# A kernel ordered by a planner: one place per batch for every stage, batches 0 to 2 in two groups, six result places, five for bt

## The chip, the cores and the metric

The kernel runs on one core of one Trainium2 chip. The metric is its device time in microseconds (us), the median of several runs. The core's engines have queues of their own and meet through semaphores: PE (TensorE) multiplies matrices, ACT (ScalarE), DVE (VectorE) and POOL (GpSimd) work on elements, SP (SyncE) issues all transfers between memory (HBM) and the core's buffers. Every queue is worked off in its order: an instruction that waits holds all that stand behind it on the same engine.

## The reference

Two attention steps with 32 inducing points, and a feed-forward stage whose nonlinearity is `h - tanh(h)`:

```python
def mab(q, kv):
    s = scale * (q @ kv.transpose(0, 2, 1))
    s = s - s.max(-1, keepdims=True)
    a = np.exp(s)
    a /= a.sum(-1, keepdims=True) + 1e-09
    return a @ kv
h = mab(I, x)                       # I: 32 x 128, for each of B = 4 batches; x: 4 x 12480 x 128
attn = mab(x, h)                    # 4 x 12480 x 128
...
h = x @ w_in                        # x: attn as 49920 x 128; w_in: 128 x 2048
g = h - np.tanh(h)
return (g @ w_out).astype(np.float32)   # w_out: 2048 x 128
```

Inputs and output are float32, but for `w_in` and `w_out`, which are 64-bit floats.

## The kernel before, in words

**Tiling.** A batch's 12480 rows are cut into seven tiles, s = 0 to 6: six of 1920 rows (four segments of 480, one for each quarter of the 128 partitions) and a last one of 960. `x` is in memory twice, transposed (`xT`, a load of 128 x 1920) and as rows (`xn`, a load of 128 x 1920; the last half tile comes from `xl` with 64 partitions). An input tile is 960 KB, half a result tile 480 KB.

**First stage of a batch** (`first`, `attend`). For each tile: load `xT`; scores against the inducing points on PE (L322, `ps_m<-xT,indT_sb`); on DVE a copy into `s1` with the row's maximum (L348). When all tiles of a group are done, the maximum is turned and spread (L355 to L367, the last writes `nb`). Then for each tile: exponential on ACT (L398), 32 x 32 transposes on DVE (L402, `et`), and 15 small matmuls that accumulate `h` in the PSUM tile `bank` (L409, `bank<-xn,et`). The rows `xn` of a tile are loaded (L391), or, for the tiles in `TURNED`, made on PE from `xT` (L381) and copied by ACT (L387): no transfer, but the same buffer. A batch that `SPLIT` names is worked in two groups of tiles, each with its own maximum, which are put together at the end with a few more small steps (`hA`, `f`); otherwise all seven tiles are one group, and no exponential starts before the last tile's maximum. At the end the sums are taken (L449), `h` is normed and folded (L465 or L461, L468) and copied to `hT` (L470).

**The map of a batch** (`linear`). The feed-forward stage is brought down to one 32 x 128 map for each batch, kept four times in `P4`: `hT` times `w_in` (L491), a copy to `M4` (L494), turned and centred (L503), a series and squares, `W` times `w_out` (L545), fold (L549), copy to `P4` (L551). Bounds are kept beside, and `bound` (the guard) decides at the end by them whether this was exact enough (`limit`); if not, a general path would run, which it doesn't here.

**Second stage** (`second`, `b_chain`). For each tile: scores against `hT` on PE (L322, `ps_m<-xT,hT`), transposes on DVE into `be` (L594), maximum (L596), difference on POOL (L601), exponential on ACT (L603), on POOL the two halves' sum into `bs` (L608), on DVE the sum (L611) and its reciprocal (L614), product on POOL (L615), transposes into `bt` (L618), on PE the matmuls with `P4` (L643, `o<-bt,P`), two copies out of PSUM (L649, into `ot` on ACT; for the last batch into an `xT` place, on ACT or DVE), and two stores (L653).

**The weights.** `w_in` and `w_out` come as four pieces each into `xn` places (L277) and are made float32 there by steps on DVE (L281 to L298), ACT (L284, L295) and POOL (L302).

**The order.** Nothing is scheduled at run time. `Plan.add` records each step with an engine, a cost, the buffers that it reads and writes, and a priority `pri`; `Plan.order` plays the program through with these costs: an engine that is free takes the ready step of the lowest priority whose buffers have a free place (`PLACES` says how many each kind has). The result is written out as the fixed order of each engine. So the numbers in `ORD`, `PLACES`, `SPLIT`, `TURNED`, the lags and the costs set where every instruction stands. `FILL` says how much of PE's idle time in the plan is filled with matmuls of no use (L734, `bank<-ident`).

In `ORD`, `first` and `second` are the starting priorities of each batch's two stages, `fs` and `ss` the step from tile to tile, `lx` and `ln` how far the loads of `xT` and `xn` go ahead, `lns` their step, `turn` and `keep` the place of the turned tiles, `base`, `q`, `half` and `late` that of the maximum, the exponentials, the end of the first stage and the bounds, `store` that of the result stores.

## Time and profile before

| what | us |
|---|---|
| median of 3 runs (220.1 to 221.13) | 220.41 |
| the profiled execution's own time | 221.32 |
| its span, first to last instruction | 219.6 |
| PE busy, with weight loads apart | 178.1 (81%) |
| DVE busy | 155.3 (71%) |
| ACT busy | 116.8 (53%) |
| POOL busy | 97.8 (45%) |

HBM reads are 47.46 MB and writes 25.56 MB, 333 GB/s over the span. The granted TensorE clock is 0.911 of full speed on average.

In what follows, PEclk is the share of full TensorE clock that was granted, in tenths for each of 40 slices of the span; the DMA line is the busy share of the 16 DMA engines in the same slices. A timeline row has its start in us, its length in us, engine, line, operation, what it writes and reads, the count, and in brackets the engine's idle time before it with what ended that. PEld is PE's weight loads, which run beside the matmuls. "SPq" is the issue of a transfer on SP, not the transfer.

### The profile page before, as it was taken

The page shows a single profiled execution, that of the slowest core. Times are in us where ns is not written, and L with a number is a line of the kernel's source. Part 1 is how long each engine was busy: PE and PEld are TensorE (multiplying, and loading weights), DVE is VectorE, ACT ScalarE, POOL GpSimd, SP SyncE. Part 2 cuts the span into 40 slices and gives each one's busy share as a digit, 9 for nine tenths or more (in the row PEclk, how much of TensorE's full clock was granted, in tenths as well). Part 3 has the DMA queues.
Part 4 walks back from the last instruction along what each step waited for, and adds up shares of the span by engine and source line. Part 5 has one row for each costly group of instructions (what it writes and reads, how often), then busy time and mean ns, then how long its engine had stood idle before and what let it go on. Part 6 is the DMA issues. An engine that isn't in the chain of part 4 may idle for free.

```text
span 219.6 us, 5239 instructions
## 1 busy us (share of the span) xinstructions
PE 178.1 (81%) x2015; PEld 92.7 (42%) x2015; DVE 155.3 (71%) x402; ACT 116.8 (53%) x229; POOL 97.8 (45%) x138
## 2 busy tenths in 40 slices
PE   7565589848968999995799985998997999799740
PEld 7542244744432467332226651334454434346310
DVE  5799986543697995667388953496979048888960
ACT  2426356930324999385178961367943836648310
POOL 1135414000299643339454641189334245989600
PEclk9979679999999999999699995799999559889995
DMA  5999998799999899999999999599999924609793
GB/s 170 414 417 357 322 405 323 268 292 344 417 421 417 262 416 363 423 405 427 416 411 323 336 419 420 192 358 421 361 381 353 378 113 179 237 36 372 286 400 125
DMA packets 15472, 73.44 MB, mean 334 GB/s; under 512 B 1872, under 2 KB 1872, under 8 KB 15440
## 3 DMA queue, kind: packets, MB, share of 16 engines
q1 hardware_dynamic: 15440, 73.03, 87.3%
q8 instruction: 18, 0.29, 0.5%
q14 instruction: 14, 0.11, 0.2%
HBM read 47.46 MB, written 25.56 MB: 333 GB/s over the span
## 4 chain that ended last, share of the span: by engine, by line
PE 46%; DMA 25%; DVE 12%; ACT 6%; POOL 4%; issue 2%; SPq 1%; ACTq 0%; POOLq 0%; DVEq 0%
PE ps_m L322 17%; DMA xT<-in_xT 14%; PE o L643 10%; PE bank L409 6%; PE ps_m L381 5%; DMA outT<-ot 4%; DMA xn<-in_xl 4%; DMA xn<-in_w_out 3%; PE ps_m L491 2%; ACT xn L387 2%; DVE xT L649 2%; ACT s L398 2%; DVE xn L292 1%; DVE xn L298 1%; PE ps_m L549 1%
## 5 line engine op out<-in xcount | busy, mean ns | idle before, releaser
L601 POOL TENSOR_TENSOR be<-be,bmx 128x480 f32<-128x480 f32 (+1 forms) x25 | 25.2, 1013 | 49.3 <-DVE bmx L596 42.6
L322 PE MATMUL ps_m<-xT,indT_sb 128*32 128x480 f32 x208 | 32.6, 667 | 17.8 <-DMA xT<-in_xT 11.5
L649 ACT COPY ot<-o 128x960 f32<-128x960 f32 x39 | 36.4, 959 | 14.7 <-DMA outT<-ot 7.9
L643 PE MATMUL o<-bt,P 32*128 32x480 f32 x184 | 31.9, 654 | 3.6 <-ACT ot L649 2.9
L615 POOL TENSOR_TENSOR be<-be,brs 128x480 f32<-128x480 f32 (+1 forms) x25 | 24.8, 995 | 21.6 <-DVE brs L614 15.3
L409 PE MATMUL bank<-xn,et 128*32 128x128 f32 (+1 forms) x840 | 30.9, 280 | 4.3 <-DMA xn<-in_xn 2.9
L348 DVE TENSOR_SCALAR_CACHE_REDUCE s<-ps_m 128x480 f32<-128x480 f32 (+1 forms) x28 | 18.2, 650 | 20.4 <-PE ps_m L322 20.4
L409 PEld LDWEIGHTS bank<-xn,et 128*32 128x32 f32 (+1 forms) x840 | 23.8, 111 | 14.5 <-issue 5.9
L322 PE MATMUL ps_m<-xT,hT 128*32 128x480 f32 x208 | 28.0, 604 | 0.2 <-ACT D L507 0.2
L387 ACT COPY xn<-ps_m 128x512 f32<-128x512 f32 (+1 forms) x32 | 17.3, 556 | 11.6 <-PE ps_m L381 11.5
L608 POOL TENSOR_TENSOR bs<-be 128x240 f32<-128x240 f32 (+1 forms) x25 | 17.9, 718 | 10.5 <-ACT be L603 10.4
L734 PE MATMUL bank<-ident 128*128 128x128 f32 x110 | 20.2, 328 | 1.9 <-POOL ident masks.py:199 1.4
L402 DVE STREAM_TRANSPOSE et<-s 128x480 f32<-128x480 f32 (+1 forms) x28 | 18.4, 659 | 3.8 <-ACT s L398 3.8
L594 DVE STREAM_TRANSPOSE be<-ps_m 128x480 f32<-128x480 f32 (+1 forms) x25 | 16.5, 661 | 5.7 <-PE ps_m L322 5.7
L734 PEld LDWEIGHTS bank<-ident 128*128 128x128 f32 x110 | 17.6, 236 | 6.8 <-issue 4.5
L381 PE MATMUL ps_m<-ident,xT 128*128 128x128 f32 x120 | 19.5, 300 | 0.7 <-ACT xn L387 0.5
L398 ACT ACTIVATE s<-s,nb 128x480 f32<-128x480 f32 (+1 forms) x28 | 19.4, 696 | 0.7 <-DVE nb L367 0.5
L381 PEld LDWEIGHTS ps_m<-ident,xT 128*128 128x128 f32 x120 | 14.2, 152 | 10.5 <-issue 3.0
L618 DVE STREAM_TRANSPOSE bt<-be 128x480 f32<-128x480 f32 (+1 forms) x25 | 16.6, 664 | 2.3 <-POOL be L615 2.1
L603 ACT ACTIVATE be<-be 128x480 f32<-128x480 f32 (+1 forms) x25 | 14.9, 604 | 3.9 <-POOL be L601 3.9
L322 PEld LDWEIGHTS ps_m<-xT,indT_sb 128*32 128x32 f32 x208 | 5.8, 117 | 26.0 <-issue 10.9
L596 DVE TENSOR_REDUCE bmx<-be 128x15 f32<-128x480 f32 (+1 forms) x25 | 15.7, 633 | 0.1
(126 smaller groups left out, 226.8 us busy)
## 6 DMA issues: line engine op xcount, KB each, us to landing
xT<-in_xT SPq DMA_DIRECT2D x24, 960.0 KB, 9.3
outT<-ot SPq DMA_DIRECT2D x39, 480.0 KB, 8.6
xn<-in_xn SPq DMA_DIRECT2D x16, 960.0 KB, 10.2
outT<-xT SPq DMA_DIRECT2D x13, 480.0 KB, 3.1
xn<-in_w_in SPq DMA_DIRECT2D x4, 512.0 KB, 5.4
xn<-in_w_out SPq DMA_DIRECT2D x4, 512.0 KB, 6.0
xT<-in_xT SPq DMA_DIRECT2D x4, 480.0 KB, 10.4
xn<-in_xl SPq DMA_DIRECT2D x4, 480.0 KB, 8.1
```

The source lines that it names most:

```text
L322: nc.tensor.matmul(ps[q * m:(q + 1) * m, :SEG], lhsT=w, rhs=row, start=True, stop=True)
L348: nc.vector.tensor_scalar(out=s1.get()[:P, s, :], in0=ps.get()[:P, :SEG], scalar1=1.0, scalar2=None, op0=ALU.mult, op1=ALU.max, accum_out= ...
L381: nc.tensor.transpose(out=pt.get()[:, i * 128:(i + 1) * 128], in_=xT_b[b, s].get()[:, (k + i) * 128:(k + i + 1) * 128], identity=ident)
L387: nc.scalar.copy(out=x.get()[:, k:k + n, :].rearrange("p k c -> p (k c)"), in_=pt.get()[:, :n * 128])
L398: nc.scalar.activation(out=sl, in_=sl, func=AF.Exp, scale=SC, bias=nb.get()[:P], accum_out=sums.get()[:P, s:s + 1])
L402: add("DVE", 0.66, lambda et=et, s=s, P=P: nc.vector.transpose(out=et.get()[:P].rearrange("p k i -> p (k i)"), in_=s1.get()[:P, s, :]), re ...
L409: nc.tensor.matmul(hacc.get()[q * m:(q + 1) * m, :], lhsT=et.get()[:P, k, :], rhs=x.get()[:P, k, :], start=(s == group[0] and k < NQ), sto ...
L601: add("POOL", 1.02, lambda: nc.gpsimd.tensor_tensor(out=be.get()[:P], in0=be.get()[:P], in1=wide(bmx.get()[:P]), op=ALU.subtract), reads=[ ...
L615: add("POOL", 1.02, lambda: nc.gpsimd.tensor_tensor(out=be.get()[:P], in0=be.get()[:P], in1=wide(brs.get()[:P]), op=ALU.mult), reads=[brs] ...
L643: nc.tensor.matmul(tiles[q // 2].get()[:, q % 2, :SEG], lhsT=P4_b[b].get()[p, :], rhs=bt.get()[p, :], start=True, stop=True)
L649: copy(out=ot.get().rearrange("p (q n) -> p q n", q=2), in_=o.get()[:, :, :SEG])
L734: nc.tensor.matmul(bank[:, 2 * C:2 * C + 128], lhsT=ident, rhs=ident, start=first_fill, stop=True, skip_group_check=not first_fill)
```

## The change

The change gives `ORD`'s entries a value for each batch where there was one for all (`of(name, b)` reads either), and sets all numbers anew; no step of the computation is another. Beside that:

- `SPLIT`: batches 0, 1 and 2 are worked in two groups (of 4 and 3, 4 and 3, 5 and 2 tiles), batch 3 in one; before, batches 1, 2 and 3 were, and batch 0 in one.
- `TURNED`: eight tiles as before, others: none of batch 1, tiles 0 and 1 of batch 2, 0 and 3 of batch 3.
- `PLACES`: `ot` (half results) six for five, `bt` five for three, `bs` one for ten.
- `FILL` is 0.7 for 0.5, and the lag that the plan takes for loads 2.5 for 3. `PACE` is 1.0 and changes nothing.

The core of the diff:

```diff
-FILL = 0.5
-PLACES = dict(xT=10, xn=5, s1=1, be=5, bt=3, et=3, ot=5, ps=3, o=2, bs=10, D=1, M4=1, P1=2, P4=2)
...
-ORD = dict(first=(-45, 295, 470, 815), second=(630, 840, 935, 580), fs=15, ss=23, lx=-271, ln=-96, lns=3, turn=61,
...
-SPLIT = {1: 5, 2: 4, 3: 5}
-IN_LAG, OUT_LAG = 3, 1.7
+FILL = 0.7
+PLACES = dict(xT=10, xn=5, s1=1, be=5, bt=5, et=3, ot=6, ps=3, o=2, bs=1, D=1, M4=1, P1=2, P4=2)
...
+ORD = dict(first=(-155, 195, 380, 915), second=(430, 815, 820, 935), fs=(16, 24, 10, 6), ss=(56, 54, 79, 44),
...
+TURNED = {(0, 0), (0, 2), (0, 3), (0, 4), (2, 0), (2, 1), (3, 0), (3, 3)}
+
+SPLIT = {0: 4, 1: 4, 2: 5}
+IN_LAG, OUT_LAG = 2.5, 1.7
...
+    def of(name, b):
+        v = ORD[name]
+        return v[b] if isinstance(v, tuple) else v
...
-            add("PE", 0.96, pe, reads=[x, ind_b, s1], writes=[ps], pri=pri + ORD["fs"] * s)
+            add("PE", 0.96, pe, reads=[x, ind_b, s1], writes=[ps], pri=pri + of("fs", b) * s)
```

What that does to the engines' queues is seen in their order. The lines of the changed kernel are 5 to 9 higher (L391 becomes L400, L649 becomes L658).

SP, the loads of the start in the kernel before: `w_in` and `w_out` into `xn` places, `xT` of batches 0 and 1, and from the first `in_xn` on the rows of batch 0 (two tiles and the last, `in_xl`) and of batch 1.

```order
L277 DMA xn<-in_w_in 128x1024 x4
L277 DMA xn<-in_w_out 128x1024
L337 DMA xT<-in_xT 128x1920 x2
L277 DMA xn<-in_w_out 128x1024
L337 DMA xT<-in_xT 128x1920 x2
L277 DMA xn<-in_w_out 128x1024 x2
L337 DMA xT<-in_xT 128x1920 x2
L337 DMA xT<-in_xT 128x960
L337 DMA xT<-in_xT 128x1920 x2
L391 DMA xn<-in_xn 128x1920
L337 DMA xT<-in_xT 128x1920
L391 DMA xn<-in_xn 128x1920
```

The same stretch of SP's queue in the change:

```order
L282 DMA xn<-in_w_in 128x1024 x4
L346 DMA xT<-in_xT 128x1920 x6
L400 DMA xn<-in_xn 128x1920
L346 DMA xT<-in_xT 128x960
L282 DMA xn<-in_w_out 128x1024
L346 DMA xT<-in_xT 128x1920
L282 DMA xn<-in_w_out 128x1024
L346 DMA xT<-in_xT 128x1920
L400 DMA xn<-in_xn 128x1920
L400 DMA xn<-in_xl 64x1920
L346 DMA xT<-in_xT 128x1920
L282 DMA xn<-in_w_out 128x1024 x2
```

All of batch 0's `xT` now goes ahead of `w_out`, and `xl` of batch 0, which stood behind all of `w_out`, three tiles of batch 1 and the second row tile (the next row after the first fence), goes ahead of the third tile of batch 1 and of half of `w_out`.

PE before, at the end of batch 2's first stage: L409 the last accumulation (`xn_1421`), L643 a result of batch 1, L468 and L491 the way to `hT_2` and from it, `xT_1563` and `xT_1607` tiles 1 and 2 of batch 3 (scores against `indT`), `xT_738` tile 0 of batch 2.

```order
L409 MATMUL bank_92<-xn_1421,et_1561 32x128 x15
L643 MATMUL o_1634<-bt_1584,P4_1282 128x480 x2
L643 MATMUL o_1637<-bt_1584,P4_1282 128x480 x2
L468 MATMUL ps_m_1645<-fold_71,P1_1640 128x32
L322 MATMUL ps_m_1654<-xT_1563,indT_sb_74 32x480 x4
L491 MATMUL ps_m_1665<-win_sb_75,hT_2_79 32x512 x4
L322 MATMUL ps_m_1674<-xT_1607,indT_sb_74 32x480 x4
L322 MATMUL ps_m_1684<-xT_738,hT_2_79 32x480 x4
L503 MATMUL ps_m_1690<-cen_73,M4_1679 128x132 x2
```

The same place in the change, where tiles 1 and 2 of batch 3 are `xT_1572` and `xT_1615`, and tiles 0 and 1 of batch 2 `xT_778` and `xT_805`:

```order
L477 MATMUL ps_m_1649<-fold_71,P1_1634 128x32
L331 MATMUL ps_m_1656<-xT_1572,indT_sb_74 32x480 x4
L500 MATMUL ps_m_1666<-win_sb_75,hT_2_79 32x512 x4
L331 MATMUL ps_m_1673<-xT_778,hT_2_79 32x480 x4
L331 MATMUL ps_m_1684<-xT_805,hT_2_79 32x480 x4
L512 MATMUL ps_m_1695<-cen_73,M4_1680 128x132 x2
L512 MATMUL ps_m_1698<-cen_73,M4_1680 128x132 x2
L652 MATMUL o_1707<-bt_1574,P4_1290 128x480 x2
L652 MATMUL o_1710<-bt_1574,P4_1290 128x480 x2
L331 MATMUL ps_m_1723<-xT_1615,indT_sb_74 32x480 x4
```

Tile 1 of batch 3 still stands ahead of L491 of batch 2; tile 2 has gone behind two scores and a result.

ACT before, around batch 3's last accumulation: exponentials of the second stage (`be`), copies of results into `ot`, L662 of the guard, L494 the copy to `M4` of batch 3.

```order
L649 COPY ot_2078<-o_2036 128x960
L649 COPY ot_2090<-o_2039 128x960
L459 ACTIVATE hA_2083<-hA_2083,f_2065 128x128
L603 ACTIVATE be_2045<-be_2045 128x480
L649 COPY ot_2145<-o_2115 128x960
L649 COPY ot_2152<-o_2118 128x960
L603 ACTIVATE be_2122<-be_2122 64x480
L662 ACTIVATE xT_2173<-wout_sb_76 128x1024
L662 ACTIVATE xT_2183<-wout_sb_76 128x1024
L494 COPY M4_2193<-ps_m_2175 128x512
```

The same in the change; L407 are the last two exponentials of batch 3, L503 the copy to `M4`.

```order
L658 COPY ot_2042<-o_2009 128x960
L407 ACTIVATE s1_1540,sum_1543<-s1_1540,nb_1934 128x480
L658 COPY ot_2083<-o_2012 128x960
L407 ACTIVATE s1_1540,sum_1543<-s1_1540,nb_1934 64x480
L612 ACTIVATE be_1982<-be_1982 128x480
L658 COPY ot_2117<-o_2089 128x960
L658 COPY ot_2124<-o_2092 128x960
L612 ACTIVATE be_2015<-be_2015 64x480
L658 COPY ot_2164<-o_2149 128x960
L658 COPY ot_2168<-o_2152 128x960
L671 ACTIVATE xT_2182<-wout_sb_76 128x1024
L503 COPY M4_2192<-ps_m_2176 128x512
```

Copies now stand between batch 3's exponentials (two more pairs of both above these rows), and four copies and one L671 ahead of `M4`. On SP the stores were not in the order of the copies before: the last three of batch 1 (`ot_1727`, `ot_1748`, `ot_1768`, copied ahead of the first results of batch 2) stood behind the last loads of batch 3, mixed with later ones. In the change all stores of this stretch are in the order of the copies, and the two stores ahead of the last two loads are those of `ot_1858` and `ot_1870`, the first two results of batch 2.

Ahead of batch 3's tile 1 there stand 17 result stores on SP where there were 19, and ahead of the last load of all 26 where there were 25. The guard's last steps (L683 to L711) now come behind nearly all work of batch 3 on DVE, and of the last batch's 13 copies four are on DVE where five were.

36 lines of the change are left out of this document (20 added, 16 removed).

## The prediction

> **What bounds the kernel now.** First the page's slices: the granted clock, the DMA engines' busy share and what they moved.
>
> ```profile
> span 219.6 us, 5239 instructions
> PEclk9979679999999999999699995799999559889995
> DMA  5999998799999899999999999599999924609793
> GB/s 170 414 417 357 322 405 323 268 292 344 417 421 417 262 416 363 423 405 427 416 411 323 336 419 420 192 358 421 361 381 353 378 113 179 237 36 372 286 400 125
> ```
>
> The DMA engines are full for most of the first 170 us and half empty after that. The windows view gives the same by stretch (columns: stretch, its length, busy time of PE, PEld, DVE, ACT and POOL, granted clock, DMA share, GB/s):
>
> ```profile
> 20.00:45.00 25.00, 19.56 (x223) 12.09 (x224) 19.09 (x41) 14.87 (x33) 7.25 (x5) 0.86 0.88 322
> 45.00:57.00 12.00, 8.52 (x151) 4.58 (x148) 4.27 (x18) 1.23 (x3) 0.00 (x0) 1.00 1.02 335
> 57.00:95.00 38.00, 34.84 (x468) 17.70 (x460) 29.65 (x83) 23.69 (x51) 21.27 (x31) 1.00 1.00 388
> 95.00:135.00 40.00, 33.22 (x439) 16.23 (x439) 28.43 (x78) 25.28 (x50) 21.50 (x31) 0.93 1.01 393
> 135.00:145.00 10.00, 10.00 (x68) 3.00 (x58) 6.00 (x13) 4.02 (x10) 2.62 (x7) 0.77 0.76 272
> 145.00:168.00 23.00, 21.42 (x318) 10.88 (x319) 19.36 (x54) 14.28 (x31) 13.46 (x19) 1.00 1.00 376
> 168.00:182.00 14.00, 11.53 (x100) 4.99 (x90) 4.60 (x12) 8.08 (x11) 5.36 (x7) 0.63 0.64 257
> 182.00:213.00 31.00, 26.19 (x222) 12.85 (x214) 27.72 (x63) 16.77 (x30) 21.57 (x31) 0.94 0.64 254
> ```
>
> A well-fed queue moves 388 to 393 GB/s over 78 us. I take 390, or 0.39 MB a us, as what it can do. Below that are 20 to 57 and 135 to 168: there the queue waits for work. After 168 no load is left: 182 to 213 is bound by VectorE (27.72 of 31 us). So the time is the landing of batch 3's last load, and the tail behind it. The transfers' sizes, from the page's part 6:
>
> ```profile
> xT<-in_xT SPq DMA_DIRECT2D x24, 960.0 KB, 9.3
> outT<-ot SPq DMA_DIRECT2D x39, 480.0 KB, 8.6
> ```
>
> That is 0.98 MB (2.5 us at 390) for an input tile and 0.49 MB (1.3 us) for half a result tile.
>
> **Part 1: batch 0 in two groups, w_out behind it.** Rows of the timeline for batch 0:
>
> ```profile
> 31.50 0.65 DVE L348 TENSOR_SCALAR_CACHE_REDUCE s<-ps_m 128x480 f32<-128x480 f32 x1
> ...
> 39.11 0.16 DVE L367 TENSOR_SCALAR nb<-ps_m 128x1 f32<-128x1 f32 x1 [0.80 <-PE ps_m L365]
> ...
> 41.00 1.07 PE L409 MATMUL bank<-xn,et 128*32 128x128 f32 x30 [0.60 <-DVE et L402]
> ...
> 51.96 1.07 PE L409 MATMUL bank<-xn,et 64*32 64x128 f32 x30 [0.58 <-DMA xn<-in_xl]
> ...
> 54.62 0.18 DVE L470 COPY hT<-ps_m 128x32 f32<-128x32 f32 x1
> ...
> 66.09 1.01 PE L322 MATMUL ps_m<-xT,indT_sb 128*32 128x480 f32 x8 [0.68 <-DMA xT<-in_xT]
> ```
>
> The maximum of all seven tiles (39.11) stands ahead of the first accumulation (41.00), and the xn places come free only there, so loads of xn wait. In the change four tiles are enough. Their fourth is done at 31.50 with VectorE's w_out steps mixed in; with w_in's alone I put the first accumulation near 30, an estimate (between 25, some 4 us after the fourth tile's landing by the sizes above, and 41, no gain). In the queue the last piece of batch 0 has 14.0 MB up to it where it had 16.0 (the transfers' sizes added in the order shown above): 5.1 us at 390. So hT of batch 0, 54.62, comes about 5 us earlier, and with it the load of b1's tile 3, which SyncE issues once a tile of batch 0 has been scored a second time.
>
> What is that worth at the end? The two stretches from 20 to 57 moved 25 x 0.322 + 12 x 0.335 = 12.07 MB; at 390 that takes 30.9 us instead of 37. The most is -6.1. Against it stands a new stop: the second w_out load takes the place of b0's turned tile 0, so it waits for that first accumulation, and on SyncE's queue all other loads wait behind it. The 11.0 MB ahead are through at about 13 + 7.9 / 0.39 = 33 (b0's first tile lands just before the first scores at 13, row below), so with an issue at 30 the queue just holds; for an issue at 33, a load into an empty queue takes at least 4.1 us to land against 1.3 in the stream (the second row below is that of the loads into xn in the first 60 us).
>
> ```profile
> 12.98 1.52 PE L322 MATMUL ps_m<-xT,indT_sb 128*32 128x480 f32 x8 [4.45 <-DMA xT<-in_xT]
> ...
> DMA to landing us min/median/max: 4.1/7.0/12.4
> ```
>
> I take 2 of these 2.8 us. Part 1: **-4.1** (bounds -6.1 and +1).
>
> GpSimd's w_out steps now fall beside batch 0's chain:
>
> ```profile
> 9.15 0.42 DVE L281 TENSOR_SCALAR xn<-xn 128x512 uint32<-128x512 uint32 x1
> ...
> 10.53 1.27 DVE L281 TENSOR_SCALAR xn<-xn 128x512 uint32<-128x512 uint32 x1 [0.36 <-DMA xn<-in_w_out]
> 10.25 1.26 POOL L302 TENSOR_TENSOR win_sb<-win_sb,xn 128x512 f32<-128x512 f32 x1 [8.96 <-DVE xn L298]
> ```
>
> The same VectorE step took 0.42 us alone and 1.27 beside a GpSimd multiply. Four such multiplies, each holding VectorE 0.85 us longer, are at most 3.4 us, but in before, too, all eight lie on VectorE's path; inside the 2 us above. The Trainium skill, "SBUF — State Buffer", "Who interferes with whom", calls this an exclusive lock: the later of the two waits for the whole instruction. The rows agree (10.53 + 1.27 is the multiply's end plus 0.3). By that rule taken fully, Part 1 would be -0.7 instead of -4.1.
>
> **Part 2: batch 2 to batch 3.** PE's queue between batch 2's sums and its hT:
>
> ```profile
> 130.52 0.41 PE L468 MATMUL ps_m<-fold,P 128*128 128x32 f32 x2
> 134.01 1.83 PE L322 MATMUL ps_m<-xT,indT_sb 128*32 128x480 f32 x8 [3.08 <-DMA xT<-in_xT]
> 135.61 1.93 PE L491 MATMUL ps_m<-win_sb,hT 128*32 128x512 f32 x8
> ...
> 140.33 6.13 SPq L337 DMA_DIRECT2D xT<-in_xT  x4
> ```
>
> b3's tile 1 stands ahead of batch 2's second stage and its data come 3.08 us late; PE is then at half speed (1.83 and 1.93, against 1.01 for scores at 66.09). b3's tile 3 can be loaded only at 140.33, and 135 to 145 runs at 272 GB/s. In the change two result stores fewer (2.5 us) are ahead of that tile 1, and b3's tile 2 (1.83 us) goes behind two scores of batch 2. So the issue at 140.33 comes 4 us earlier against the stream, which covers the hole: 2.72 MB at 390 are 7.0 us, -3.0; 145 to 168 has 8.65 MB, 22.2 us, -0.8. I take **-2.5** (0 to -3.8). One store more stands ahead of the last load: **+1.3**.
>
> **Part 3: six result places, stores in the order of the copies.** The rows around the last load (the row on landing is that load's own):
>
> ```profile
> 145.28 0.94 ACT L649 COPY ot<-o 128x960 f32<-128x960 f32 x1
> ...
> 159.63 0.47 SPq L391 DMA_DIRECT2D xn<-in_xl  x1
> DMA to landing us min/median/max: 8.7/8.7/8.7
> ...
> 169.63 0.96 ACT L649 COPY ot<-o 128x960 f32<-128x960 f32 x1 [3.71 <-DMA outT<-ot]
> 170.64 3.12 PE L643 MATMUL o<-bt,P 32*128 32x480 f32 x8 [1.94 <-ACT ot L649]
> 173.69 1.92 PE L409 MATMUL bank<-xn,et 64*32 64x128 f32 x30
> 175.21 1.99 ACT L662 ACTIVATE xT<-wout_sb 128x1024 f32<-128x1024 f32 x2
> 179.06 1.81 PE L491 MATMUL ps_m<-win_sb,hT 128*32 128x512 f32 x8
> 180.94 0.59 ACT L494 COPY M<-ps_m 128x512 f32<-128x512 f32 x1 [3.74 <-PE ps_m L491]
> ```
>
> The load lands at 159.63 + 8.7 = 168.3, but its accumulation runs at 173.69: three results copied by 146 are stored behind the last loads and hold three of five places, so ScalarE waits 3.71 us, PE's results wait for it, and the last accumulation stands behind them at half clock. The copy to M is at 180.94, 12.6 us after the landing. In the change the copies that stand ahead of the last accumulation need only stores issued before the last loads. Behind it ScalarE makes four more copies before M, which need the four stores behind the load: the fourth lands 4 x 1.3 = 5.0 us after it, then one copy (0.96) and one of the two L662 (1.0): 7.0 us. **-5.6** (bounds: -7.5 if half of those stores are in time, 0 if the wait only moves). Late on that path next is PE (sums, hT, L491), whose accumulation, results and L491 (1.92, half of 3.12, 1.81 at half clock) and the small steps between just fill the 7 us.
>
> **Part 4: the tail.** After the copy to M the same work remains, bound by VectorE.
>
> ```profile
> 201.53 1.60 PE L734 MATMUL bank<-ident 128*128 128x128 f32 x12
> 211.76 1.16 DVE L649 COPY xT<-o 128x960 f32<-128x960 f32 x1 [0.37 <-PE o L643]
> ```
>
> One of the five copies on VectorE (1.16) goes to ScalarE, and the guard's steps go last, under the last store. FILL 0.7 puts six fill matmuls (a run of x12 is 1.60 us) ahead of several results: up to 3.2 us more on PE for two of them that nothing hides. bs with one place makes GpSimd wait for VectorE's L611; two of those sums stand side by side on GpSimd only once, in batch 0, so 0; bt's two more places cost nothing. The two groups' extra small steps for batch 0 are those that batch 3 no longer has. I take **0** (-1.5 to +3.2).
>
> **The sum.** -4.1 - 2.5 + 1.3 - 5.6 + 0 = -10.9. The profiled execution took 221.32 us (span 219.6 and 1.7 around it); it becomes 210.4. The median of the runs is 220.41, 0.9 below it: **209.5 us**.
>
> **Rivals.** (a) The early gain is eaten: PE is busy 34.84 of 38 us in 57 to 95, so a batch that starts earlier may only wait for PE. Then Parts 1 and 2 give nothing: 220.4 + 1.3 - 5.6 = 216. Against: in 95 to 135 PE still waits for data (3.08 at 134.01).
>
> (b) The queue never runs dry and Part 4 gains: -6.1 - 3.8 + 1.3 - 7.5 - 1.5 = -17.6, 203; more likely short of it, to 206.
>
> (c) Slower: copies between batch 3's exponentials. Without a split in batch 3, ScalarE has four copies among its seven exponentials. If each waits for a store as at 169.63 (3.71), the last accumulation, and all behind it, comes up to 4 x 3.71 = 14.8 us later, less the some 3 us by which the exponentials would be ahead: +12 on 209.5, 221.5. It decides from three such waits on. Against: their places need stores ahead of the last loads; for: 3.71 was seen with the same kind of order.
>
> (d) The waits only change places: 0 to -1 us, 220.
>
> (e) The Trainium skill, "DMA: Bandwidth & Descriptors", "Where 436 GB/s comes from", puts a core's HBM share near 358 GB/s. By 358 in place of 390 Part 1 would be 12.07 / 0.358 = 33.7, so -3.3 + 2; Part 2 -1.6; the store ahead +1.4; Part 3 -5.2; and the time 214. The rows of 388 and 393 over 78 us do not bear it out; 3 in 100 of (a)'s side.
>
> **Numbers.** Forecast (206 to 213) 0.50; (a) with (e) 0.23; (b) 0.13; (c) 0.09; (d) 0.05. Range 203 to 218: it leaves out (c), (d) and a little of (a) and (b). Measurements of this kernel (220.1 to 221.13) tell no less than 0.5%, 1.1 us, from no change. Faster 0.50 + 0.23 + 0.13 = 0.86, same 0.05, slower 0.09.
>
> **What would show it.** Right: the first L367 before 30 and hT of batch 0 before 50; 20 to 57 above 350 GB/s; no hole at b3's tile 3; the last accumulation within 2 us of its load, with no long wait of ScalarE for a store. Wrong: SyncE's queue dry at the second w_out load; the last load landing no earlier than 168; ScalarE waiting between batch 3's exponentials; PE at half clock in the tail.

## The result, and the profile after

The changed kernel takes 213.7 us (median of six executions, 210.33 to 215.59); the kernel before, in the same set, 220.25 (218.8 to 221.71). The ratio is 0.963, with a 95% interval of 0.954 to 0.972: faster, inside the range of the prediction and 4 us above its forecast. It lies just above the band of the forecast (206 to 213) and beside the times of two of its rivals (214 for (e), 216 for (a)), so the number alone does not tell them apart. Medians here are over all executions; ratios leave out executions over 1.5% above their kernel's fastest, so the two can differ by a per cent, and ot7warm, of which one execution is left, has no ratio.

The profiled execution of the changed kernel took 210.33 us, against 221.32 of the one before: 11.0 less, where the sum of the prediction was 10.9. That agreement flatters the sum: this execution is the fastest of its six, and a second profiled execution (below) took 217.11. Both are needed to see which terms hold.

The page's slices after:

```profile
span 208.6 us, 5319 instructions
PEclk9979999856999999999999999999999999999995
DMA  5999999999699999999999999999999996547890
GB/s 169 410 426 424 406 377 397 197 402 413 211 395 424 420 313 339 424 410 415 422 416 373 330 295 422 412 361 371 426 416 359 366 415 268 215 189 317 334 390 17
```

The windows view after, by the stretches shown of before (same columns: PE, PEld, DVE, ACT, POOL, granted clock, DMA share, GB/s):

```profile
20.00:45.00 25.00, 20.77 (x311) 14.74 (x311) 14.20 (x43) 12.79 (x30) 3.89 (x3) 0.90 1.02 353
45.00:57.00 12.00, 11.52 (x76) 4.75 (x79) 9.87 (x25) 4.64 (x12) 2.75 (x3) 0.79 0.84 326
57.00:95.00 38.00, 34.16 (x458) 17.89 (x450) 29.21 (x84) 22.44 (x48) 21.67 (x32) 1.00 1.01 390
95.00:135.00 40.00, 33.39 (x457) 17.00 (x459) 28.87 (x78) 24.89 (x50) 21.10 (x32) 1.00 1.01 384
135.00:145.00 10.00, 7.80 (x90) 2.69 (x90) 9.15 (x23) 5.90 (x14) 9.39 (x18) 1.00 1.00 364
145.00:168.00 23.00, 21.22 (x318) 12.05 (x312) 15.41 (x37) 17.25 (x32) 10.20 (x12) 1.00 1.02 393
168.00:182.00 14.00, 13.10 (x124) 5.10 (x121) 10.92 (x24) 10.01 (x21) 9.02 (x14) 1.00 0.74 301
```

The dry stretch from 20 to 45 is filled (share 1.02 for 0.88), but a new one stands at 45 to 57 (0.84 for 1.02). Together the two moved 25 x 0.353 + 12 x 0.326 = 12.74 MB, against 12.07 before: 0.67 MB more, or 1.7 us at 390 GB/s. The one at 135 to 145 is closed (364 GB/s for 272), and from 168 to 182 the clock is whole (1.00 for 0.63).

Batch 0 in the timeline after (L376 was L367, L418 was L409, L400 is a row load, L346 a tile load):

```profile
24.34 0.15 DVE L376 TENSOR_SCALAR nb<-ps_m 128x1 f32<-128x1 f32 x1
...
27.12 1.07 PE L418 MATMUL bank<-xn,et 128*32 128x128 f32 x30
...
42.39 1.92 PE L418 MATMUL bank<-xn,et 64*32 64x128 f32 x30 [0.29 <-DMA xn<-in_xl]
...
45.19 5.03 PE L331 MATMUL ps_m<-xT,indT_sb 128*32 128x480 f32 x24
...
50.59 0.19 DVE L479 COPY hT<-ps_m 128x32 f32<-128x32 f32 x1 [0.84 <-PE ps_m L477]
...
53.47 0.33 SPq L400 DMA_DIRECT2D xn<-in_xn  x1
...
56.08 3.43 SPq L346 DMA_DIRECT2D xT<-in_xT  x4
```

The first accumulation is at 27.12 instead of 41.00, the last of batch 0 at 42.39 instead of 51.96. Then batch 1's first three scores run at half clock (5.03 us for what takes 2.6 elsewhere) in front of the last steps to batch 0's hT. It comes at 50.59, 4.0 us earlier than before. A row load waits on SyncE's queue until 53.47, when everything issued ahead of it has nearly landed (53.95): this is the dry stretch.

The last loads and what follows, in the timeline after (L400 at 155.46 the last full row load, at 157.14 batch 3's last load, which lands 7.2 us later, at 164.33):

```profile
151.42 0.11 DVE L376 TENSOR_SCALAR nb<-ps_m 128x1 f32<-128x1 f32 x1
...
154.36 1.05 PE L418 MATMUL bank<-xn,et 128*32 128x128 f32 x30
...
155.46 0.34 SPq L400 DMA_DIRECT2D xn<-in_xn  x1
...
157.14 0.47 SPq L400 DMA_DIRECT2D xn<-in_xl  x1
...
164.41 1.07 PE L418 MATMUL bank<-xn,et 64*32 64x128 f32 x30
...
166.55 2.24 PE L652 MATMUL o<-bt,P 32*128 32x480 f32 x8 [1.06 <-ACT ot L658]
...
169.27 0.96 ACT L658 COPY ot<-o 128x960 f32<-128x960 f32 x1 [0.28 <-DMA outT<-ot]
170.13 1.06 ACT L671 ACTIVATE xT<-wout_sb 128x1024 f32<-128x1024 f32 x1
171.09 0.58 ACT L503 COPY M<-ps_m 128x512 f32<-128x512 f32 x1
```

The last accumulation runs within 0.1 us of its load (before: 5.3 us behind it), and the copy to M stands 6.8 us behind the landing instead of 12.6. The fourth store behind the load lands at 169.17, 4.8 us after it; one copy and one L671 follow, and then M. What is left of ScalarE's wait for a store costs PE 1.06 us at 166.55.

### The profile page after: what moved, and what is told of

Same layout as the page of the kernel before. It is cut to its first block, busy times and chain, and to the rows that moved or that the text cites. A ratio compares the mean times of both kernels' runs of the same rounds, so it can differ in the third digit from the quotient of the medians.

```text
span 208.6 us, 5319 instructions
## 1 busy us (share of the span) xinstructions
PE 175.4 (84%) x2055; PEld 96.7 (46%) x2055; DVE 150.7 (72%) x392; ACT 118.0 (57%) x230; POOL 96.7 (46%) x138
## 4 chain that ended last, share of the span: by engine, by line
PE 35%; DMA 34%; DVE 15%; ACT 6%; POOL 4%; issue 2%; SPq 1%; ACTq 0%; DVEq 0%; POOLq 0%
DMA xT<-in_xT 13%; PE ps_m L331 12%; PE o L652 9%; DMA outT<-ot 6%; DMA xn<-in_xl 4%; DMA xn<-in_w_out 4%; PE bank L743 4%; DMA xn<-in_xn 4%; PE bank L418 3%; ACT s L407 3%; DVE xn L297 2%; DMA xn<-in_w_in 2%; PE ps_m L390 2%; ACT ot L658 2%; DVE xn L303 2%
## 5 line engine op out<-in xcount | busy, mean ns | idle before, releaser
L658 ACT COPY ot<-o 128x960 f32<-128x960 f32 x39 | 36.5, 958 | 12.6 <-PE o L652 6.9
L331 PE MATMUL ps_m<-xT,indT_sb 128*32 128x480 f32 x208 | 30.5, 635 | 11.0 <-DMA xT<-in_xT 9.2
L418 PE MATMUL bank<-xn,et 128*32 128x128 f32 (+1 forms) x840 | 32.0, 285 | 5.7 <-DMA xn<-in_xn 3.7
L418 PEld LDWEIGHTS bank<-xn,et 128*32 128x32 f32 (+1 forms) x840 | 25.0, 113 | 13.6 <-DVE et L411 3.7
L652 PE MATMUL o<-bt,P 32*128 32x480 f32 x184 | 29.3, 613 | 1.2 <-ACT ot L658 1.1
L331 PE MATMUL ps_m<-xT,hT 128*32 128x480 f32 x208 | 26.9, 571 | 0.7 <-DVE be L603 0.5
L743 PE MATMUL bank<-ident 128*128 128x128 f32 x150 | 23.4, 305 | 1.4 <-POOL ident masks.py:199 1.4
L396 ACT COPY xn<-ps_m 128x512 f32<-128x512 f32 (+1 forms) x32 | 17.1, 561 | 12.6 <-PE ps_m L390 12.4
L743 PEld LDWEIGHTS bank<-ident 128*128 128x128 f32 x150 | 20.5, 212 | 6.2 <-issue 4.8
L407 ACT ACTIVATE s<-s,nb 128x480 f32<-128x480 f32 (+1 forms) x28 | 19.5, 698 | 3.2 <-DVE nb L376 3.2
L390 PE MATMUL ps_m<-ident,xT 128*128 128x128 f32 x120 | 18.1, 290 | 2.3 <-DMA xT<-in_xT 1.2
L307 POOL TENSOR_TENSOR wout_sb<-wout_sb,xn 128x512 f32<-128x512 f32 x4 | 5.6, 1398 | 30.4 <-DVE xn L303 26.5
L390 PEld LDWEIGHTS ps_m<-ident,xT 128*128 128x128 f32 x120 | 13.6, 147 | 10.6 <-issue 3.0
```

The source lines that it names most:

```text
L331: nc.tensor.matmul(ps[q * m:(q + 1) * m, :SEG], lhsT=w, rhs=row, start=True, stop=True)
L390: nc.tensor.transpose(out=pt.get()[:, i * 128:(i + 1) * 128], in_=xT_b[b, s].get()[:, (k + i) * 128:(k + i + 1) * 128], identity=ident)
L407: nc.scalar.activation(out=sl, in_=sl, func=AF.Exp, scale=SC, bias=nb.get()[:P], accum_out=sums.get()[:P, s:s + 1])
L418: nc.tensor.matmul(hacc.get()[q * m:(q + 1) * m, :], lhsT=et.get()[:P, k, :], rhs=x.get()[:P, k, :], start=(s == group[0] and k < NQ), sto ...
L652: nc.tensor.matmul(tiles[q // 2].get()[:, q % 2, :SEG], lhsT=P4_b[b].get()[p, :], rhs=bt.get()[p, :], start=True, stop=True)
L658: copy(out=ot.get().rearrange("p (q n) -> p q n", q=2), in_=o.get()[:, :, :SEG])
```

## The experiments

Twelve kernels, in three sets of four; each set has its own executions of the kernel before (medians 220.59, 220.14 and 220.29). For the edits to an engine's order, `behind(ops, moved, anchor)` puts operations of the planner's finished list, with what needs them, right behind another; `ahead` puts them right in front. Everything else keeps its place. The helpers shift the line numbers of these kernels, so the tiles' names tell the operations.

All traces beside each other, in us. "s6 to row load" is the time from the landing of batch 3's last tile to the issue of its last full row load; "landing to M" from the landing of batch 3's last load to the copy to M; "M to end" from there to the end of the span. Each row is one profiled execution; median and ratio are those of the kernel's own set.

| kernel | median | ratio (95%) | hT b0 | hT b2 | s6 to row load | last load lands | landing to M | M to end |
|---|---|---|---|---|---|---|---|---|
| before | 220.25 | 1 | 54.6 | 131.0 | 6.8 | 168.4 | 12.6 | 38.6 |
| changed | 213.7 | 0.963 (0.954 to 0.972) | 50.6 | 129.4 | 9.6 | 164.3 | 6.8 | 37.5 |
| again | 217.55 | 0.980 (0.967 to 0.992) | 50.1 | 129.5 | 11.1 | 167.5 | 8.8 | 39.0 |
| nofill | 218.81 | 0.993 (0.987 to 0.999) | 49.1 | 129.5 | 9.6 | 163.7 | 8.7 | 39.7 |
| guardup | 215.68 | 0.975 (0.966 to 0.985) | 50.5 | 130.1 | 9.3 | 167.2 | 8.9 | 38.9 |
| hT0 | 220.85 | 1.004 (0.997 to 1.010) | 51.5 | 130.8 | 11.2 | 167.1 | 8.5 | 38.7 |
| b_ot6 | 217.19 | 0.978 (0.970 to 0.987) | 57.1 | 132.8 | 6.8 | 168.6 | 9.1 | 38.7 |
| b_stores | 221.13 | 0.990 (0.980 to 1.000) | 58.8 | 134.1 | 5.4 | 176.1 | 7.6 | 38.7 |
| b_pe23 | 216.8 | 0.988 (0.982 to 0.994) | 53.9 | 130.0 | 5.0 | 162.6 | 12.9 | 38.8 |
| ot7 | 212.59 | 0.955 (0.944 to 0.965) | 48.9 | 130.8 | 11.2 | 167.9 | 6.5 | 38.6 |
| b_both | 216.23 | 0.971 (0.962 to 0.981) | 56.5 | 133.6 | 5.0 | 166.2 | 10.2 | 38.7 |
| skip02 | 212.37 | 0.967 (0.961 to 0.972) | 50.3 | 128.4 | 11.3 | 164.8 | 7.9 | 38.5 |
| ot7warm | 217.46 | none | 51.0 | 131.0 | 8.8 | 169.9 | 11.3 | 39.0 |
| best | 214.56 | 0.973 (0.967 to 0.978) | 47.5 | 131.1 | 9.6 | 164.9 | 8.5 | 38.1 |

**The changed kernel once more (again).** No edit.

> The changed kernel once more, nothing edited. Theory: its median lies again some 6 to 7 us below the kernel before (213 to 214 against 220), and its executions spread from 210 to 216, wider than those before. If 210.33 was the rule and the others the exceptions, the median comes at 210 to 211. The second profile is to show where a longer execution loses its time: theory A, in the first 60 us, where TensorE runs at half clock and the queue is dry; theory B, in the tail behind batch 3's last load.

Median 217.55 against 220.59 (213.36 to 220.5 over six): less gained than in the first set, and less than expected. The executions spread over 10 us in the two sets; those of the kernel before spread over 3 us in the first and 6 in the second, but for one of 268 us. The second profile is 6.8 us longer in its span. At hT of batch 2 the two traces are level (129.4 and 129.5), so theory A, the first 60 us, has no part in it; the last load lands 3.1 us later, which neither theory named; the way to M is 2.1 longer and the tail 1.6, which is theory B. In the timeline of this run, behind its last load (landing 167.46):

```profile
168.75 0.96 ACT L658 COPY ot<-o 128x960 f32<-128x960 f32 x1 [2.79 <-DMA outT<-ot]
...
169.76 3.01 PE L652 MATMUL o<-bt,P 32*128 32x480 f32 x8 [1.19 <-ACT ot L658]
...
174.28 1.94 PE L500 MATMUL ps_m<-win_sb,hT 128*32 128x512 f32 x8
...
176.28 0.59 ACT L503 COPY M<-ps_m 128x512 f32<-128x512 f32 x1 [1.51 <-PE ps_m L500]
```

and its windows:

```profile
135.00:145.00 10.00, 8.78 (x94) 3.53 (x93) 9.33 (x21) 5.69 (x15) 8.44 (x17) 1.00 1.00 323
145.00:168.00 23.00, 20.33 (x302) 11.27 (x306) 14.95 (x40) 15.80 (x30) 10.37 (x13) 0.93 0.92 353
168.00:182.00 14.00, 12.74 (x89) 5.05 (x80) 6.01 (x14) 9.08 (x16) 4.64 (x7) 0.76 0.73 295
```

The same store wait as in the first trace (a copy released at 168.75, PE idle for 1.19 us) is here followed by half clock: L500 takes 1.94 us instead of 1.07. The first trace had an idle time of 1.06 us at the same place and kept its clock. So some 2 us lie between two outcomes of the same program, and one profile shows only one of them. That the pause decides which is not shown: with a seventh place (ot7 below) it is gone, and the clock falls all the same. The DMA engines are busy all of 135 to 145 in both traces and move 323 GB/s here, 364 there.

**No fill matmuls in the tail (nofill).**

```diff
-            for _ in range(int(FILL * gaps.get(op, 0.0) / 0.25)):
+            for _ in range(0 if op.start >= P4_b[B - 1].writer.start else int(FILL * gaps.get(op, 0.0) / 0.25)):
```

> The changed kernel without the fill matmuls behind batch 3's P4 (nothing else moves). Theory: in the tail TensorE stands on the path, and the runs of 12 and 8 fills between results (1.53 three times, 0.99, 1.09, of which the queue can use only one while it waits) put off results: 2 to 3 us less than the changed kernel. Rival: the fills only stand in gaps in which TensorE would wait for VectorE's transposes; without them the clock halves and each run of eight result matmuls takes 2.0 instead of 1.1: no gain, or up to 2 us more.

Median 218.81, 1.3 us above the unedited kernel of the same set, with ratios whose intervals overlap (0.987 to 0.999 and 0.967 to 0.992): no gain, so the rival. Its windows:

```profile
182.00:208.00 26.00, 16.48 (x114) 6.23 (x106) 19.18 (x48) 12.11 (x18) 15.73 (x22) 0.81 0.68 269
```

The clock is 0.81 here, 0.92 and 1.00 with the fills, and M to end is 39.7 us, the longest of the table. So the fills, though they stand on the chain that ended last, cost nothing here that leaving them out gives back; that they pay is not told from no change.

**The guard ahead of the last piece (guardup).**

```diff
+    smin_op, turn_op, decide_op = bound_ops
+    ops = ahead(ops, [smin_op], bt_last)
+    ops = behind(ops, [out_last], turn_op)
+    ops = behind(ops, [copy_last], decide_op)
```

> The changed kernel with the guard's last three steps (smallest sum, turn, decision) ahead of the last piece's transpose, results and copy. Theory: the end is set by the guard: the limit is written at 202.1, and TensorE's branch behind it, 3.76 us, ends 3.3 us after the last store has landed; with the limit some 1.8 us earlier the time falls by 1.5 to 2 us. Rival: the last piece comes as much later as the guard comes earlier, and the branch waits for the store in any case: no change, within 0.5 us.

Median 215.68 against 217.55, ratios 0.975 and 0.980 with intervals that overlap: no gain that can be told, and M to end is 38.9 against 39.0. In the timeline:

```profile
207.65 0.14 DVE L759 TENSOR_SCALAR limit<-low 1x1 f32<-1x1 f32 x1
207.76 1.16 DVE L697 COPY xT<-o 128x960 f32<-128x960 f32 x1
```

and the last store by itself (the view of one source line):

```profile
L701 SPq DMA_DIRECT2D outT<-xT x1: 332/332/332, 208.9 to 208.9; - x1
...
DMA to landing us min/median/max: 4.3/4.3/4.3
```

The limit is early enough, but the last copy is as much later, and its store now takes 4.3 us to land instead of 2.7 (207.44 to 210.14 in the second profile of the changed kernel). The end falls 1.7 us behind that store instead of 5.2: the rival, M to end being the same to a tenth.

**Batch 1's first scores behind batch 0's steps to hT and L500 (hT0).**

```diff
+    ops = behind(ops, [PE scores of batch 1, tiles 0 to 2], up0)      # up0: L500 of batch 0
```

> The changed kernel with batch 1's first three scores behind batch 0's second stage (L477, L500) on TensorE, and VectorE's first maximum of batch 1 behind them. Theory: these scores, 5.03 us at half clock, hold up hT of batch 0 (50.6) and with it the third and fourth w_out steps on VectorE; hT comes at 46 to 48, the fourth row load of batch 1 is issued near 50 instead of 53.5, batch 1's tile 3 near 52.5 instead of 56.1, the dry stretch of the queue shrinks, and the end comes 2 to 3 us earlier. Rival: the early gain is eaten by TensorE, which is busy nine tenths of the time from 57 on: end unchanged within 0.5 us, with TensorE waiting for nothing earlier than now.

3.3 us slower than the unedited kernel by the medians, and by a test that was not the one meant. In the timeline:

```profile
47.67 3.68 PE L784 MATMUL bank<-ident 128*128 128x128 f32 x16 [3.56 <-DVE P L509]
...
56.87 0.33 SPq L439 DMA_DIRECT2D xn<-in_xn  x1
```

The planner fills the hole that the scores left with 16 fill matmuls, which hold up hT just as long, and the third w_out step now waits for the scores. The row load goes out at 56.87 instead of 53.27. So this is a delay of 3.4 to 3.6 us at 57, and it comes through to the end: 3.3 us by the medians, and the ratio's interval (0.997 to 1.010) lies above the unedited kernel's (0.967 to 0.992).

**The sixth place alone (b_ot6), on the kernel before.**

```diff
-        return Buf(lambda: io.tile(shape, F32, name=tag, bufs=PLACES[tag]), tag)
+        return Buf(lambda: io.tile(shape, F32, name=tag, bufs=PLACES[tag] + (tag == "ot")), tag)
-    bs_tiles = [io.tile([128, KB, m // 2 + 1], F32, name=f"bs_{k}", bufs=1) for k in range(PLACES["bs"])]
+    bs_tiles = [io.tile([128, KB, m // 2 + 1], F32, name=f"bs_{k}", bufs=1) for k in range(6)]
```

> The kernel before with one more place for half results (six; bs has six places instead of ten for the room) and every engine's order as it was: the place of Part 3 without its order of stores. Theory: ScalarE's copies at 162.16 and 169.63 no longer wait 3.16 and 3.71 for stores; the last accumulation, 173.69, runs within 1 us of its load's landing, the copy to M comes 7 to 8 us behind the landing instead of 12.6, and the time falls by 4 to 5.6 us. Rival: the wait only moves to the next copies, and the copy to M stays 12 us behind the landing: no change within 1 us.

Median 217.19 against 220.14, ratio 0.978. The timeline around the last load (landing 168.58):

```profile
162.95 0.96 ACT L649 COPY ot<-o 128x960 f32<-128x960 f32 x1 [0.33 <-DMA outT<-ot]
...
169.76 0.96 ACT L649 COPY ot<-o 128x960 f32<-128x960 f32 x1 [3.06 <-DMA outT<-ot]
...
171.77 1.07 PE L409 MATMUL bank<-xn,et 64*32 64x128 f32 x30
...
177.68 0.59 ACT L494 COPY M<-ps_m 128x512 f32<-128x512 f32 x1 [1.92 <-PE ps_m L491]
```

Between the two theories: the first wait (3.16) is gone, the second (3.71) has moved one copy on and is 3.06. M stands 9.1 us behind the landing, 3.5 better, at whole clock for the last accumulation (1.07 for 1.92). All of it reaches the end, since M to end is 38.6 and 38.7.

**The order of stores alone (b_stores), on the kernel before.**

```diff
+    held = [held[2], held[3], held[6]]      # stores of the three results copied by 146
+    ops = behind(ops, [the loads and stores of SP from batch 3's first row load on, without held], ready)
```

> The kernel before with the three results that were copied by 146 stored ahead of batch 3's row loads instead of behind its last load: the order of stores of Part 3 without its sixth place. Theory: the last load lands up to 3.8 us later (three stores, 1.47 MB at 0.39 a us), but ScalarE's 3.71 us wait goes and the copy to M stands 7 us behind the landing: -5.6 + 3.8, about -2 us, and to -4 where the stores fill the dry stretch of the queue from 135 to 145. Rival: no wait goes, only the load comes later: +2 to +4.

Median 221.13 against 220.14; the ratio's interval (0.980 to 1.000) ends at no change. The timeline behind the last load (landing 176.11):

```profile
179.10 1.82 ACT L688 COPY ot<-o 128x960 f32<-128x960 f32 x2 [5.97 <-issue]
...
182.56 1.06 PE L530 MATMUL ps_m<-win_sb,hT 128*32 128x512 f32 x8
183.70 0.58 ACT L533 COPY M<-ps_m 128x512 f32<-128x512 f32 x1 [0.39 <-PE ps_m L530]
```

No copy waits for a store any more, and M stands 7.6 us behind the landing: the wait does go, 5.0 of the 5.6 that the term had. But the load lands 7.7 us later. Of these, 3.1 were there at hT of batch 2 already (134.1 against 131.0), the other 4.6 are about the three stores ahead of it (3.8 by the expectation). In the kernel before, the order pays with one hand what it takes with the other. The change reaches its order with one store more ahead of the last load (26 for 25), this kernel with three (28).

**Part 2 alone (b_pe23), on the kernel before.**

```diff
+    ops = behind(ops, [PE scores of batch 3, tiles 1 and 2], third second score of batch 2)
```

> The kernel before with batch 3's tiles 1 and 2 scored on TensorE (and their maxima taken on VectorE) behind batch 2's second stage and its first three second scores: Part 2 by itself. Theory: L491 of batch 2 comes 3 to 4 us earlier, batch 3's tile 3 is issued near 136 instead of 140.33, the stretch from 135 to 145 moves 350 GB/s instead of 272, the last load lands 2 to 3 us earlier, and the time falls by as much. Rival: TensorE or the store waits behind the last load take it up: the load comes earlier and the end does not.

Median 216.8 against 220.14, 3.3 less; ratio 0.988, 2.7 us. Its window:

```profile
135.00:145.00 10.00, 8.64 (x98) 3.04 (x90) 7.37 (x19) 4.34 (x9) 5.70 (x15) 1.00 1.02 422
```

The stretch is full (422 GB/s for 272), batch 3's tile 3 is issued at 132.7 instead of 140.3, and the last load lands at 162.6, earlier than in any run of the changed kernel. The way to M stays long (12.9): the two parts work apart, as the theory had it. It is a stronger edit than the change's own, which leaves tile 1 where it was, puts tile 2 behind two scores, and has two stores fewer ahead.

**Both (b_both): the sixth place and Part 2 on the kernel before.** The two edits above together.

> The kernel before with Part 2 (batch 3's tiles 1 and 2 scored behind batch 2's second scores) and the sixth place for half results together; batch 0, the order of stores and the tail as before. Theory: the two add up, since one brings the last load earlier (162.6 instead of 168.4) and the other shortens the way from that landing to the copy to M: 3.3 + 3.0, some 6 us below the kernel before, 214. Then the changed kernel (213.7 and 217.6 in its two sets) gets nothing more from batch 0's two groups, which is rival (a) of the prediction for Part 1 alone. If Part 1 is worth its 4 us, the changed kernel is some 3 to 4 us faster than this one. Rival: one waits for the other: 217, as each alone.

Median 216.23 against 220.29, ratio 0.971. By ratio 6.4 us, where the two alone give 4.8 and 2.7; by median 4.1, where they give 3.0 and 3.3. So they add up for the most part. Beside the changed kernel's two sets (0.963 and 0.980, intervals that both overlap this one) it is level: batch 0's two groups, the stores' order and the rest of the change together bring nothing on top that these runs can tell.

**A seventh place (ot7), on the changed kernel.**

```diff
-        return Buf(lambda: io.tile(shape, F32, name=tag, bufs=PLACES[tag]), tag)
+        return Buf(lambda: io.tile(shape, F32, name=tag, bufs=PLACES[tag] + (tag == "ot") - (tag == "bt")), tag)
```

> The changed kernel with a seventh place for half results (bt has four instead of five for the room), every engine's order as it was. Theory: what is left of Part 3's wait, ScalarE's 2.79 us at 168.75 in the second look at the changed kernel, leaves TensorE idle for 1.2 us behind the last accumulation and at half clock until 178; with a seventh place both go, the copy to M comes 6 us behind the landing of the last load instead of 8.7, and the median falls by 2 to 3 us, with the clock at 1.00 in the 14 us behind the landing. Rival: TensorE halves there for another reason (it has little to do until the second stage is through): the clock stays at half and nothing is gained.

Median 212.59 against 220.14, ratio 0.955 (0.944 to 0.965): the fastest kernel of this study by ratio, ahead of the changed kernel's second set and not told apart from its first. The timeline (landing 167.89):

```profile
167.93 1.07 PE L418 MATMUL bank<-xn,et 64*32 64x128 f32 x30 [0.83 <-DMA xn<-in_xl]
...
168.94 0.96 ACT L658 COPY ot<-o 128x960 f32<-128x960 f32 x1 [2.12 <-DMA outT<-ot]
...
172.40 1.94 PE L500 MATMUL ps_m<-win_sb,hT 128*32 128x512 f32 x8
```

PE no longer idles behind the last accumulation, and M comes 6.5 us behind the landing instead of 8.8. The clock, however, falls all the same (L500 again 1.94), behind a wait of 0.83 us for the load: the place was right, the promise of a whole clock was not.

**Two result stores left out (skip02), on the changed kernel.**

```diff
-                add("SP", 1.2, lambda ot=ot, at=at: nc.sync.dma_start(out=outT[:, at:at + 2 * SEG], in_=ot.get()),
+                add("SP", 1.2, lambda ot=ot, at=at: None if (b, s) == (0, 2) else nc.sync.dma_start(out=outT[:, at:at + 2 * SEG], in_=ot.get()),
```

> The changed kernel without the two result stores of batch 0's tile 2 (0.98 MB; this part of the output is left out), which stand in the queue near 77 us; nothing else differs. Theory: the queue sets the end, so the 2.5 us that the two stores take at 0.39 MB a us come off the end. Rival: TensorE sets it from 57 to 95 (34.16 of 38 us busy): the loads of batches 1 and 2 land 2.5 us earlier, wait for places, and nothing is left of it at batch 3's last load.

Median 212.37, ratio 0.967 (0.961 to 0.972). The ratio is between those of the changed kernel's two sets, the median 1.3 and 5.2 us below theirs. In its trace 1.0 of the 2.5 us is left at hT of batch 2 (128.4), and the last load lands at 164.8, against 164.3 and 167.5. Two sets of one kernel that lie 3.9 us apart cannot tell a gain of 2.5 us from none: this leaves the theory and the rival open.

**A seventh place and a busy PE (ot7warm).**

```diff
             for k in range(len(groups)):
+                for _ in range(7 if b == B - 1 else 1):
                     nc.tensor.matmul(ps3.get()[:, :1], lhsT=fold2, rhs=sms.get()[:, k:k + 1], start=(k == 0), stop=(k == len(groups) - 1))
```

> The changed kernel with the seventh place for half results (bt has four), and batch 3's one-column sums matmul (L458) written seven times instead of once, into the same place with the same value, so that TensorE works through 1.2 us more of its wait for the last load. Theory: with the place alone TensorE still waited 0.83 us for that load and was at half clock from 171 to 175 (L500 1.94, L331 2.01 for half as many); without a pause in front of the last accumulation the clock stays at 1.00 and the copy to M comes 5.5 instead of 6.5 us behind the landing: 1 to 2 us less than with the place alone (212.6). Rival: the clock falls all the same, and seven matmuls are 1 us more on TensorE where the load is early: no change or +1.

Median 217.46, 4.9 above the seventh place alone in the set before. The two sets of the changed kernel itself lie 3.9 apart, so how much of this the edit costs stays open; it gains nothing that shows. The profiled execution took 222.01:

```profile
168.81 2.02 PE L418 MATMUL bank<-xn,et 128*32 128x128 f32 x30 [2.18 <-DMA xn<-in_xn]
170.76 3.15 PE L459 MATMUL ps_m<-sm,fold 128*128 128x1 f32 x14
173.84 1.92 PE L418 MATMUL bank<-xn,et 64*32 64x128 f32 x30
```

The wait is here one load earlier, for the full row load, in front of the matmuls that were to bridge it. The clock is down before they start, and they take 3.15 us on the path, with the last load there since 169.9. In this execution it is the rival, and worse than it said.

**That, and an earlier hT of batch 0 (best).** This kernel has the seventh place and the seven matmuls too. On VectorE, batch 0's steps to hT stand ahead of the third w_out step; on PE the three scores stand behind L500, without fills in front of it.

```diff
+    ops = ahead(ops, [what L500 of batch 0 needs], heads[6])        # heads[6]: first step of the third w_out block
+    ops = behind(ops, [PE scores of batch 1, tiles 0 to 2], up0)
```

> As the one before, and batch 0's hT earlier: on VectorE its steps stand ahead of the third w_out step (which waits for its load), on TensorE batch 1's first three scores stand behind L500 with no fill matmuls in front of it. Theory: hT of batch 0 at 46 to 47 instead of 49 to 51, batch 1's tile 3 issued 2 to 3 us earlier, the dry stretch near 54 shorter; worth 1.5 to 2.5 us at the end if the queue carries it, none if rival (a) holds. Rival: as with the scores moved alone, the w_out steps wait for batch 1's first maximum and the queue becomes dry for longer: 3 us slower.

Median 214.56, ratio 0.973: 2.9 us below ot7warm, from which it differs in this alone, and no better than the changed kernel. hT of batch 0 is 3 us earlier, as meant (the timeline, with the first step of the third w_out block behind it):

```profile
47.50 0.19 DVE L521 COPY hT<-ps_m 128x32 f32<-128x32 f32 x1 [0.79 <-PE ps_m L519]
47.60 0.42 DVE L327 TENSOR_SCALAR xn<-xn 128x512 uint32<-128x512 uint32 x1
```

But batch 1's tile 3 is issued at 56.8, no earlier than before, because SyncE's queue waits for something else (the waits of SP from 40 to 62: what, in all, times, longest):

```profile
SPq L441 <- POOL wout_sb L348: 10.5, 2, 8.3
```

GpSimd's multiply of the third w_out block gives the place for the row load free. VectorE's steps on that block now stand behind hT and begin later than in the changed kernel (47.60 for 45.75). So the edit moved the wait from one stage to the other, and by 57 the queue gained nothing: in ot7warm the same tile is issued at 56.8 too. hT of batch 2 is at 131.1, against 131.0 there. Where the 2.9 us come from stays open, and what an earlier queue is worth was not tried by this.

## Why the prediction came out as it did

The first trace fits the sum in total: last load -4.0 (predicted -4.1 - 2.5 + 1.3 = -5.3), landing to M -5.8 (-5.6), tail -1.1 (0), together -11.0 before rounding. The second gives -0.9, -3.8 and +0.4, -4.2. By medians the change is worth 6.6 us in one set and 3.0 in the other, not 10.9. That the first trace hits the sum is luck: it is the fastest of twelve executions, and in it the short gain at the last load and the tail's gain cancel. Step by step:

**Part 1 (-4.1): the steps came earlier, the queue gained less than half; the step that failed is the price of the stop.** The first accumulation came at 27 (predicted near 30) and hT of batch 0 4.0 us earlier (about 5; it just missed being before 50). But -4.1 is what the queue was to gain from 20 to 57: 6.1 if it never ran dry, less 2 for a new stop. It gained 1.7 (345 GB/s, not above 350), so 4.4 us stand where the prediction had 2. Batch 1's tile 3, whose load was to come with hT, is issued at 56.08 instead of 56.98, only 0.9 us earlier. The stop also came elsewhere: the second w_out load went out at 28.28, in time. The time was lost around batch 0's last load (204 GB/s from 36 to 40, last section) and at the row load that waits for the third w_out block's place, where nothing lands from 53.95 to 58.07. Beside GpSimd's w_out multiplies two of VectorE's steps took 1.38 us instead of 0.43 there (35.32 and 52.35); four were the most that the prediction allowed for.

From 57 to 135 the rows give 38 x 0.390 + 40 x 0.384 = 30.18 MB, against 30.46 before: 0.28 MB or 0.7 us less. So 1.0 of the 1.7 us is left at 135; as much as 0.7 may have gone the way of rival (a). Averaged over the traces, the nine kernels with the change have moved 0.5 MB more than the five without it by 57 us, and 0.8 MB more by 135. What the queue gains early is thus mostly kept, and hT0 shows the same for a loss by its medians.

hT of batch 0 misleads here. Over the five traces with batch 0 as before, it is at 56.2 on average and hT of batch 2 at 132.3; over the nine with the change, 49.9 and 130.1. Of 6.3 us, 2.2 are left. But batch 0's last load has 2.0 MB less ahead of it only because other loads were put behind it, and these still have to come. And the prediction overlooked that `TURNED` leaves batch 1 no turned tile: it has one row load more, so that up to batch 2's last load the queue carries 0.98 MB (2.5 us) more than before, and that load lands at 125.37 instead of 124.17. Among the five, whose order is the same up to there, a late hT of batch 0 (53.9 to 58.8) goes with a late hT of batch 2 (130.0 to 134.1).

**Part 2 (-2.5): right in the first trace.** From 135 to 145 it moved 0.92 MB more than before (364 GB/s for 272), 2.4 us at 390. The second trace has 323 there and 353 from 145 to 168, and most of the gain is gone by the last load; why is open. In its stronger form alone (b_pe23) the edit measured 3.3 by median and 2.7 by ratio, with the hole closed as described.

**A term that the sum lacked: batch 3 without groups.** Part 4 put the small steps of the two groups at nothing, and only rival (c) looked at what else the missing split does. In the table, the last row load is issued 5.0 to 6.8 us behind the landing of batch 3's last tile in the five kernels that split batch 3, and 8.8 to 11.3 behind it in the nine that don't. In the rows above nb, formed from all seven tiles, is at 151.42; the first accumulation is at 154.36, and the load that waits for its place at 155.46. So the tiles that Parts 1 and 2 bring 5.8 us earlier (batch 3's last lands at 145.8 instead of 151.6) give a row load only 3.0 earlier (155.46 instead of 158.43). This is read from fourteen traces of kernels that differ in batch 3's turned tiles and priorities too; a kernel that differs in this split alone wasn't tried, so that the split is the cause, and its price at the end, stay open.

**Part 3 (-5.6): the mechanism right, its size that of one outcome.** 12.6 us became 6.8 in the first trace (predicted 7.0), and by the path that was forecast: four stores behind the load, the fourth 4.8 us after it (5.0), then a copy and one L671. In the second it was 8.8, and there the last to come was PE (the 1.51 us in front of M). The prediction had put PE's path at half clock at just the 7 us; that is the term that it had too small, by 1.8, of which PE's pause for ScalarE's copy is 1.2. The experiments divide the gain: the order of stores is worth 5.0 of the way to M and costs landing, the sixth place 3.5 with no cost. In the changed kernel's order with six places L500 ran at half clock (1.94 us) in all five other traces, with 7.9 to 8.9 from landing to M; only the first trace kept its clock.

**Part 4 (0): right in sum.** From M to the end takes 37.5 to 39.7 in all fourteen traces. Inside it two steps were off: the fills (up to +3.2) are no cost that shows, since without them the tail is not shorter (39.7 us); and the guard doesn't end under the last store: the store lands at 203.67 and the span ends at 208.6. That costs nothing only because an earlier guard delays the store as much.

**The rivals.** (a) keeps a share: b_both, without batch 0's two groups, is level with the changed kernel, whose medians (213.7 and 217.55) lie on both sides of its 216. But by the rows it is mostly that the queue gained little, not that PE ate the gain. (c) did not come: between batch 3's exponentials ScalarE waits once, 0.71 us, in the first trace. (d) and (b) are out. (e) stays out by the rows, 390 and 384 GB/s over 78 us after the change, much as before; that its 214 is the first set's median is a coincidence. The Trainium skill's "DMA: Bandwidth & Descriptors", "Where 436 GB/s comes from", has 358; the trace doesn't agree with the figure.

## What to carry to other kernels

A step that comes earlier is not yet a queue that is ahead: a load that is put in front of others comes early at their cost. Count the MB that the queue has moved by a given time, and what each batch adds to it; price a new stop by all that waits behind it. Where the path behind the last transfer waits for places, count places and the order of stores together: here the place alone gave 3.5 of the 5.6 us that the two were to give, and the order alone nothing at the end that could be told, since it put stores in front of the load. A profile is one execution: where it shows PE just keeping its clock over a pause, take a second one before putting a number on that stage.

## What the runs showed of the hardware

**The clock behind a short pause.** Idle times of 1.19 (again), 0.83 (ot7) and 2.18 us (ot7warm) near the last load were followed by stretches at half clock (L500 of batch 3: 1.94 us for 1.07); an idle time of 1.06 in the first trace was not. Nor does the length of the pause decide: behind 1.08 (skip02) and 0.99 us (hT0) at the same place L500 was at half clock too. What decides was not found.

**A store beside the guard's branch.** The last store takes 2.7 us to land when the limit is written behind its issue (again, 207.44 to 210.14) and 4.3 when the limit is written ahead of it (guardup); in the kernel before, where it is ahead too, 5.0 (212.95 to 217.96). The cause was not looked for.

**Busy DMA engines that move half.** Around batch 0's last load in the changed kernel the windows view shows:

```profile
36.00:40.00 4.00, 1.75 (x37) 1.29 (x35) 3.59 (x9) 2.67 (x9) 0.42 (x1) 0.98 1.08 204
```

Share 1.08 and 204 GB/s: the full row load ahead of the 64-partition load takes 4.5 us in the stream (35.51 to 40.05) instead of 2.3, and that load itself 2.2 for half the bytes. The load ahead of batch 2's 64-partition load shows the same in the changed kernel (4.5 us, 119.36 to 123.86) and in the kernel before (4.3, 118.92 to 123.20). The cause stays open.
